# Loading the output weights of a decode kernel by transfers of 8 and 80 partitions instead of 128

## The chip, the cores and the metric

One Trainium2 chip, one of its cores. The metric is the device time of one execution in microseconds (us). The kernel before takes 1296.3 us (median; 1296.1 to 1296.4). The record sorts runs into a fast and a slow state.

## The reference, cut to what matters

One decode step of a transformer block: attention over a long cache, then a gated MLP. There are 4 sequences with one query each, 32 heads, 8192 cached positions, head size 128, model size 512, all bfloat16.

```
q = layernorm(x) @ wq                                 # 4 x 32 heads x 128
scores = q . k_cache / sqrt(128);  p = softmax(scores)
o = p . v_cache                                       # v_cache: 4 x 32 x 8192 x 128
h = x + o.reshape(4, 1, 4096) @ wo                    # wo: 4096 x 512, 4 MB
g, u = layernorm(h) @ w_gate, layernorm(h) @ w_up
h2 = h + (sigmoid(g) * u) @ w_down
```

The two caches are 512 MB together. The output weights `wo`, which the change is about, are 4 MB.

## The kernel before: the parts that matter

SyncE issues all large loads in one fixed order. K and V come in 4 MB loads into a ring of four slots, 128 partitions with 32 KB contiguous in each. `wo` reuses the buffer of the transposed keys, so it can only be loaded after the last score matmul, about 1220 us into the kernel, between the last V loads.

```
ring = SB("ring", [128, NS, TW], BF16)                 # NS = 4 slots of 32 KB per partition
kT = SB("kT", [128, 2, HT], BF16)
...
WD_PARTS = [(0, 5), (5, 10), (10, NFT)]
VL_PARTS = [(0, 64), (64, 96), (96, 128)]              # the last V load comes in three pieces
NWO = 8
HW = H // NWO                                          # 4 heads per transfer of wo
LAG2 = LAG // 2
items = [("wq", 0)]
for t in range(NT2 + LAG2):
    if t < NT2:
        items.append(("k", t))
    if t >= LAG2:
        items.append(("v", t - LAG2))
    for i in {LAG2 - 4: (0, 1), LAG2 - 3: (2, 3, 4), LAG2 - 2: (5, 6, 7)}.get(t - NT2, ()):
        items.append(("wo", i))
items += [("wg", 0), ("wu", 0), ("wd", 0)]
...
wo_v = kT[:, :, :].rearrange("p s f -> p (s f)").rearrange("p (h f) -> p h f", h=H)
...
    if kind == "wo":
        return [(lambda e: e.dma_start(
            wo_v[:, HW * t:HW * t + HW, :],
            A_wo.rearrange("(h p) f -> p h f", p=128)[:, HW * t:HW * t + HW, :]).then_inc(s_wo, 16),
            s_wo, 16 * NWO)]
...
for it in items:                                       # the order of issue on SyncE
    dma_of[it] = [P("sp", fn, (), sem, val) for fn, sem, val in load(it)]
...
# PE: all of wo but one sequence's last heads, then the last V load, then the rest
P("pe", lambda e: wo_mms(e, range(0, H - 8), 0, B, True), [otc_of[gl - 1], dma_of[("wo", NWO - 1)][0], d_xnT])
...
pe_pv(NST - 2, piece=0)
pe_pv(NST - 1, 0, 2, piece=1)
pe_pv(NST - 1, 2, 4, piece=2)
...
# wo waits for the last score matmul; the others for the last reader of their slot
op.deps = [sc_of[NST - 1]] if it[0] == "wo" else [consumed[p] for p in prev_of[it]]
```

A row of `wo` is 1 KB (512 numbers), so `wo` moves in 4096 packets of 1 KB; K and V move in packets of 32 KB.

## Time and profile before

| | |
|---|---|
| time, span of the profiled run | 1296.3 us, 1294.5 us |
| busy: DVE, PE | 48%, 39% |
| main DMA queue, share of 16 engines' span | 99.5% |
| `wo` issues | 8 of 512 KB, 32 packets on each engine |
| last V piece landed, last down-weight piece landed | 1277.4 us, 1291.1 us |

From the page of the kernel before: parts 3 (DMA queues) and 4 (the chain of waits).

```profile
q1 hardware_dynamic: 26016, 550.78, 99.5%
...
DMA 81%; PE 12%; SPq 4%; DVE 3%; issue 0%
DMA ring<-in_A_v_cache_dram 79%; PE PS L439 7%; PE PS L415 4%; SPq L220 2%; DVE kT L397 2%; SPq L236 1%; DMA ring<-in_A_wq_dram 1%; DMA ring<-in_B_w_down_dram 1%; SPq L228 1%; SPq L256 0%; PE PS L330 0%; DVE Lq L374 0%; DVE ring L347 0%; PE PS L357 0%; PE PS L637 0%
```

The kernel streams at what the DMA engines move, and 79% of its critical chain is V loads in flight. Everything that the change touches lies after 1220 us. The next view gives busy times in three stretches of that tail and one before it; the last two columns are the DMA engines' busy share and the GB/s moved.

```profile
core 0: us, PE busy (x) PEld busy (x) DVE busy (x) ACT busy (x) POOL busy (x), PEclk, DMA share, GB/s
1190.00:1220.00 30.00, 11.63 (x112) 3.73 (x116) 14.79 (x14) 0.00 (x0) 0.00 (x0) 0.56 1.01 432
1220.00:1245.00 25.00, 12.02 (x161) 5.96 (x153) 2.17 (x6) 3.62 (x7) 0.00 (x0) 0.64 0.96 390
1245.00:1270.00 25.00, 9.57 (x153) 4.59 (x154) 0.00 (x0) 0.00 (x0) 0.00 (x0) 0.50 1.01 391
1270.00:1295.00 25.00, 14.36 (x288) 9.99 (x285) 2.90 (x13) 1.91 (x4) 0.00 (x0) 0.50 0.75 286
```

The timeline of SyncE's queue before the change (start, duration of the issues, line, tiles, count). A long duration means that SyncE sat in the issue.

```profile
1220.42 0.94 SPq L220 DMA_DIRECT2D kT<-in_A_wo_dram  x2
1221.41 0.50 SPq L256 DMA_DIRECT2D ring<-in_A_v_cache_dram  x1
1221.95 22.66 SPq L220 DMA_DIRECT2D kT<-in_A_wo_dram  x3
1244.66 2.31 SPq L256 DMA_DIRECT2D ring<-in_A_v_cache_dram  x1
1247.01 6.84 SPq L220 DMA_DIRECT2D kT<-in_A_wo_dram  x3
1253.89 8.05 SPq L228 DMA_DIRECT2D ring<-in_A_v_cache_dram  x3
```

The single records of the trace add two readings. The semaphore of a 128-partition load receives 16 marks in the trace, read here as one from each engine that has finished its share: of the V load issued at 1200.9 us, seven land at 1226.6 to 1227.5, one at 1231.7 and eight at 1234.4 to 1236.4. So some engines run 8 us ahead of others. And packets have nearly fixed durations: 1.216 us for 32 KB, 46 ns for 1 KB (medians).

### The profile page before, as it was taken

The page shows a single profiled execution, that of the slowest core. Times are in us where ns is not written, and L with a number is a line of the kernel's source. Part 1 is how long each engine was busy: PE and PEld are TensorE (multiplying, and loading weights), DVE is VectorE, ACT ScalarE, POOL GpSimd, SP SyncE. Part 2 cuts the span into 40 slices and gives each one's busy share as a digit, 9 for nine tenths or more (in the row PEclk, how much of TensorE's full clock was granted, in tenths as well). Part 3 has the DMA queues.
Part 4 walks back from the last instruction along what each step waited for, and adds up shares of the span by engine and source line. Part 5 has one row for each costly group of instructions (what it writes and reads, how often), then busy time and mean ns, then how long its engine had stood idle before and what let it go on. Part 6 is the DMA issues. An engine that isn't in the chain of part 4 may idle for free.

```text
span 1294.5 us, 12693 instructions
## 1 busy us (share of the span) xinstructions
PE 499.5 (39%) x5827; PEld 193.4 (15%) x5827; DVE 625.4 (48%) x641; ACT 46.1 (4%) x102; POOL 10.6 (1%) x22
## 2 busy tenths in 40 slices
PE   3444334335244244334334334343343343343436
PEld 1011111112011021111111111011110111111114
DVE  5964644535544544535535435445535446445300
ACT  2000000000000000000000000000000000000000
POOL 3000000000000000000000000000000000000000
PEclk9996565665565565565666665665665665656655
DMA  9999999999999999999999999999999999999998
GB/s 405 434 428 432 432 428 433 431 430 430 433 431 430 433 429 431 433 427 433 434 426 434 431 427 435 429 431 435 425 434 432 426 435 428 431 434 429 429 376 322
DMA packets 26076, 551.58 MB, mean 426 GB/s; under 512 B 2340, under 2 KB 8232, under 8 KB 9256
## 3 DMA queue, kind: packets, MB, share of 16 engines
q1 hardware_dynamic: 26016, 550.78, 99.5%
q8 instruction: 45, 0.74, 0.2%
q14 instruction: 7, 0.06, 0.0%
q10 hardware_dynamic: 8, 0.00, 0.0%
HBM read 550.77 MB, written 0.00 MB: 425 GB/s over the span
## 4 chain that ended last, share of the span: by engine, by line
DMA 81%; PE 12%; SPq 4%; DVE 3%; issue 0%
DMA ring<-in_A_v_cache_dram 79%; PE PS L439 7%; PE PS L415 4%; SPq L220 2%; DVE kT L397 2%; SPq L236 1%; DMA ring<-in_A_wq_dram 1%; DMA ring<-in_B_w_down_dram 1%; SPq L228 1%; SPq L256 0%; PE PS L330 0%; DVE Lq L374 0%; DVE ring L347 0%; PE PS L357 0%; PE PS L637 0%
## 5 line engine op out<-in xcount | busy, mean ns | idle before, releaser
L397 DVE STREAM_TRANSPOSE kT<-ring 128x1024 uint32<-128x1024 uint32 x512 | 587.9, 1209 | 578.8 <-DMA ring<-in_A_k_cache_dram 578.6
L415 PE MATMUL PS<-kT,Lq 128*32 128x512 bf16 x2048 | 241.6, 619 | 563.3 <-DVE kT L397 443.8
L439 PE MATMUL PS<-ring,PTz 128*32 128x512 bf16 x2048 | 215.0, 564 | 208.7 <-DMA ring<-in_A_v_cache_dram 208.3
L415 PEld LDWEIGHTS PS<-kT,Lq 128*32 128x32 bf16 x2048 | 69.4, 135 | 692.4 <-DVE kT L397 471.9
L439 PEld LDWEIGHTS PS<-ring,PTz 128*32 128x32 bf16 x2048 | 64.5, 127 | 326.4 <-DMA ring<-in_A_v_cache_dram 197.1
L474 ACT ACTIVATE negm<-PS 128x1 f32<-128x1 f32 x16 | 2.7, 171 | 1156.3 <-PE PS L470 1156.3
L511 DVE TENSOR_SCALAR Zs<-PS,rinv 128x512 f32<-128x512 f32 x16 | 11.6, 723 | 36.4 <-PE PS L439 36.4
L506 ACT ACTIVATE PTz<-PS 64x512 bf16<-64x512 f32 x32 | 18.9, 592 | 16.5 <-PE PS L492 16.1
L518 PE MATMUL PS<-SelZ,Zs 128*128 128x8 f32 x128 | 19.1, 276 | 0.9 <-DVE Zs L511 0.9
L518 PEld LDWEIGHTS PS<-SelZ,Zs 128*128 128x128 f32 x128 | 17.6, 213 | 10.6 <-issue 8.9
L453 DVE TENSOR_REDUCE mx<-PS 128x1 f32<-128x512 f32 x16 | 10.5, 658 | 5.4 <-PE PS L415 5.4
L492 PEld LDWEIGHTS PS<-Sel,E_sb 128*32 128x32 bf16 x1024 | 10.4, 96 | 8.3 <-ACT E_sb L476 7.1
L492 PE MATMUL PS<-Sel,E_sb 128*32 128x32 bf16 x1024 | 11.0, 183 | 1.6 <-ACT E_sb L476 1.1
L476 ACT ACTIVATE E_sb<-PS,negm 128x512 bf16<-128x512 f32 x16 | 11.0, 688 | 0.5
L481 PEld LDWEIGHTS PS<-sig,Gsum 128*128 128x128 f32 x32 | 7.8, 305 | 12.6 <-issue 12.6
L481 PE MATMUL PS<-sig,Gsum 128*128 128x1 f32 x32 | 9.2, 356 | 0.0
L470 PEld LDWEIGHTS PS<-onesf,rowx 1*128 1x128 f32 x32 | 7.3, 281 | 13.0 <-issue 13.0
L470 PE MATMUL PS<-onesf,rowx 1*128 1x1 f32 x32 | 8.6, 336 | 0.0
L523 DVE CAST OT<-PS 128x8 bf16<-128x8 f32 x16 | 2.1, 132 | 11.6 <-PE PS L518 11.6
L347 DVE CAST ring<-PS 128x512 bf16<-128x512 f32 x4 | 2.5, 683 | 10.0 <-PE PS L330 10.0
L485 DVE RECIPROCAL rinv<-PS 128x1 f32<-128x1 f32 x16 | 2.1, 130 | 9.3 <-PE PS L481 9.3
L330 PE MATMUL PS<-ring,xnT 128*32 128x512 bf16 x32 | 3.6, 629 | 6.6 <-DMA ring<-in_A_wq_dram 6.6
(78 smaller groups left out, 81.3 us busy)
## 6 DMA issues: line engine op xcount, KB each, us to landing
ring<-in_A_k_cache_dram SPq DMA_DIRECT2D x64, 4096.0 KB, 29.7
ring<-in_A_v_cache_dram SPq DMA_DIRECT2D x63, 4096.0 KB, 34.0
ring<-in_A_wq_dram SPq DMA_DIRECT2D x1, 4096.0 KB, 12.3
kT<-in_A_wo_dram SPq DMA_DIRECT2D x8, 512.0 KB, 17.3
ring<-in_A_v_cache_dram SPq DMA_DIRECT2D x1, 2048.0 KB, 18.5
ring<-in_A_v_cache_dram SPq DMA_DIRECT2D x2, 1024.0 KB, 18.2
ring<-in_B_w_gate_dram SPq DMA_DIRECT2D x1, 1792.0 KB, 19.9
ring<-in_B_w_up_dram SPq DMA_DIRECT2D x1, 1792.0 KB, 23.5
```

What stands on the lines that cost most here:

```text
L220: return [(lambda e: e.dma_start(wo_v[:, HW * t:HW * t + HW, :], A_wo.rearrange("(h p) f -> p h f", p=128)[:, HW * t:HW * t + HW, :]).then ...
L228: return e.dma_start(ringv(slot)[:, c0:c1], kv_src(t, A_v_cache)[:, c0:c1]).then_inc(s_piece[i], 16)
L236: return e.dma_start(wd_v[:, t0:t1, :], B_w_down.rearrange("(t p) f -> p t f", p=128)[:, t0:t1, :]).then_inc(s_piece[3 + i], 16)
L397: return e.transpose(kT[:, buf, i * q:(i + 1) * q].bitcast(U32), ringv(src)[:, base + i * q:base + (i + 1) * q].bitcast(U32))
L415: mm = e.matmul(bS[g % 2][32 * j:32 * (j + 1), :], Lq[:, l0:l0 + 32], rhs, start=(s % GS == 0 and v == 0), stop=(s % GS == GS - 1 and v == 3),
L439: mm = e.matmul(bO[g % 2][32 * rq:32 * (rq + 1), :], PTz[:, g % 2, l0:l0 + 32], ringv(slot)[:, r0 * 128:(r0 + 4) * 128], start=(s % GS == ...
L470: p2_of[g] = P("pe", lambda e: e.matmul(bX[:, 0:1], rowx[0:1, :], onesf[0:1, 0:1], start=True, stop=True), [d2b_of[g], c_ones])
L481: L_of[g] = P("pe", lambda e: e.matmul(bX[:, 0:1], Gsum[:, :], sig[:, 0:1], start=True, stop=True), [exp_of[g], a1_of[g], d_g])
L492: mm = e.matmul(bP[g % 2][32 * a:32 * (a + 1), 32 * rr:32 * rr + 32], E_sb[:, 32 * rr:32 * rr + 32], Sel[:, a, :], start=True, stop=True, ...
L506: return e.activation(dst, src, ACT.Copy)
L511: z_of[g] = P("dve", lambda e: e.tensor_scalar(Zs[:, :], bO[g % 2][:, :], rinv[:, g % 2:g % 2 + 1], None, op0=ALU.mult), [pv_of[g * GS + G ...
L518: mm = e.matmul(bX[:, 256:264], Zs[:, 128 * r:128 * (r + 1)], SelZ[:, r, :], start=(r == 0), stop=(r == 3))
```

## The change

As its text and numbers suggest, the intent is to give one half of the engines more of `wo` than the other: 80 partitions are five shares of 16, while a transfer of 8 partitions can use 8 engines only.

```diff
-        NWO = 8
-        HW = H // NWO
+
+        WO_PARTS = [(0, 80, 8 * i, 8 * i + 8) for i in range(4)] + [(p, p + 8, 0, H) for p in range(80, 128, 8)]
+        NWO = len(WO_PARTS)
         LAG2 = LAG // 2
@@
-            for i in {LAG2 - 4: (0, 1), LAG2 - 3: (2, 3, 4), LAG2 - 2: (5, 6, 7)}.get(t - NT2, ()):
+            for i in {LAG2 - 4: (0, 1), LAG2 - 3: (2, 3, 4, 5, 6), LAG2 - 2: (7, 8, 9)}.get(t - NT2, ()):
@@
             if kind == "wo":
+                p0, p1, h0, h1 = WO_PARTS[t]
                 return [(lambda e: e.dma_start(
-                    wo_v[:, HW * t:HW * t + HW, :],
-                    A_wo.rearrange("(h p) f -> p h f", p=128)[:, HW * t:HW * t + HW, :]).then_inc(s_wo, 16),
+                    wo_v[p0:p1, h0:h1, :],
+                    A_wo.rearrange("(h p) f -> p h f", p=128)[p0:p1, h0:h1, :]).then_inc(s_wo, 16),
                     s_wo, 16 * NWO)]
```

Bytes, packets and everything on the other engines stay the same. Four transfers now move partitions 0 to 79 (8 heads each), six move 8 neighbouring partitions with all 32 heads.

## The prediction

> **What bounds it.** DMA throughput. Queue table: one queue takes 99.5% of 16 engines' span. Chain of waits: 81% DMA, 79% V loads. A 32 KB packet takes 1.213 to 1.22 us, so each DMA engine moves 27 GB/s, back to back. DVE (48%) and PE (39%) wait.
>
> Only the last 75 us can change. The 16 completion marks of each load, in the trace, show two groups of engines: of the V load issued at 1200.9 us, seven land at 1226.6-1227.5, one at 1231.7, eight at 1234.4-1236.4. In the tail the early group lacks work: busy engines drop from 16 to 9 at 1242-1245 (about 35 engine-us), because SyncE sits in the issue of output-weight transfers (11.3 us at 1221.95, 10.1 us at 1234.5 in the timeline). The last down-weight transfer ends at 1287 on the early eight, at 1289.4-1291.1 on the late eight; the kernel ends 3.3 us later.
>
> **What changes.** Same bytes; 8 issues become 10. Before, each engine moves 256 packets of 1 KB at 46 ns: 11.8 us. The Trainium skill, "DMA: Bandwidth & Descriptors", "Why a DMA increments its semaphore by 16 and not by 1", says the engine count is the largest one up to 16 that divides the outer dimension, the lowest-numbered. The 4-partition load of x fits in this trace: 4 data packets. So 80 partitions use 16 engines (160 packets each, 7.4 us), 8 partitions only engines 0-7 (192 more, 8.8 us). Engines 0-7: 16.2 us (+4.4). Engines 8-15: 7.4 us (-4.4). The intent must be that 0-7 are the early group, whose 8 us lead equals the difference (80% sure; no view numbers the engines). By engine time alone the idle gap fills, both groups end near 1287.5, and the gain is 3-4 us.
>
> **Against it.** The Trainium skill, "SBUF — State Buffer", "Door 1: The DMA port swizzle", says four adjacent partitions share one of 16 ports of 27.2 GB/s. No run here shows it yet. Each 8-partition transfer then puts four engines on each of two ports: 128 KB per port, 4.7 us instead of 1.47 us. Those ports (partitions 80-127) also take the late engines' V writes, and while engines 0-7 queue at two ports, their own stand idle. Six transfers: 17.6 us if the engines of a port stagger (two runs of three, six steps of 1.47 us each), 28 us in lockstep. With the 7.4 us that is 25 to 36 us for engines 0-7 instead of 11.8: +13 to +24. Less the idle gap (4.7 us), plus about 3 us for sharing with V: their end goes from 1287 to 1298-1309, past the old 1291.1. All of it is on the critical path: every later load on these engines (last V pieces, gate, up, down) queues behind it.
>
> **Prediction: 1304 us (+0.6%), 8 in 10 within 1293 to 1318. Faster by over 2%: 0.01; within 2%: 0.92; slower by over 2%: 0.07.**
>
> **What shows it.**
> - Unchanged until about 1220 us.
> - 8-partition transfers land 8 marks, not 16.
> - 1 KB packets take 100-190 ns while those transfers run; if 46 ns, the port argument is wrong and the time is near 1293.
> - The groups swap: engines with extra packets end last; GB/s in the last slices falls below 376 and 322.
> - The last V pieces land 5-15 us later than 1272-1277.
>
> **What would make it wrong.** No port limit, or buffering hides it: 1292-1294. Engines 0-7 are the late group: 1300 without port sharing, 1310-1320 with it. SyncE's blocked issues can move either way.

## The result

| | before | after |
|---|---|---|
| time, median | 1296.3 us | 1332.2 us (1329.2 to 1333.4, 4 runs) |
| ratio, 95% interval | | 1.0274 (1.0256 to 1.0291) |
| last mark of the last V piece | 1277.4 us | 1313.8 us |
| last mark of the down weights | 1291.1 us | 1327.4 us |
| median duration of a 32 KB packet, 1226 to 1263 us | 1.216 us | 1.938 us |
| median duration of a 1 KB packet, 1226 to 1300 us | 47 ns | 95 ns |

A ratio is the mean time of one kernel's fast runs over that of the other's of the same rounds, so it is not quite the ratio of the medians quoted.

The change made the kernel slower by 2.7%, outside the predicted range of 1293 to 1318 us. The 36 us are all there when the last V piece lands (1313.8 against 1277.4); what follows it is as long as before. The same stretches after the change, and one more:

```profile
1190.00:1220.00 30.00, 12.44 (x112) 3.89 (x116) 14.65 (x14) 0.00 (x0) 0.00 (x0) 0.56 1.00 431
1220.00:1245.00 25.00, 11.74 (x156) 5.18 (x149) 2.00 (x5) 3.62 (x7) 0.00 (x0) 0.57 1.06 298
1245.00:1270.00 25.00, 4.86 (x38) 2.24 (x38) 0.17 (x1) 0.00 (x0) 0.00 (x0) 0.56 0.92 189
1270.00:1295.00 25.00, 0.00 (x0) 0.00 (x0) 0.00 (x0) 0.00 (x0) 0.00 (x0) 0.50 0.80 198
1295.00:1331.00 36.00, 20.07 (x403) 13.54 (x403) 2.90 (x13) 1.91 (x4) 0.00 (x0) 0.50 0.75 265
```

The first line is as before. In the second the DMA engines are *more* busy than before (1.06 against 0.96) and move *less* (298 GB/s against 390). A busy DMA engine is one with a packet open; it says nothing of the rate. In the third the rate is half of before, and in the fourth PE has nothing to do for 25 us.

SyncE's queue after the change:

```profile
1220.31 0.89 SPq L222 DMA_DIRECT2D kT<-in_A_wo_dram  x2
1221.25 0.51 SPq L258 DMA_DIRECT2D ring<-in_A_v_cache_dram  x1
1221.81 41.74 SPq L222 DMA_DIRECT2D kT<-in_A_wo_dram  x5
1263.59 2.96 SPq L258 DMA_DIRECT2D ring<-in_A_v_cache_dram  x1
1266.59 23.33 SPq L222 DMA_DIRECT2D kT<-in_A_wo_dram  x3
1289.96 2.14 SPq L230 DMA_DIRECT2D ring<-in_A_v_cache_dram  x3
```

SyncE sits 41.7 us in five issues and 23.3 us in three, where before it had sat 22.7 us in three and 6.8 us in three. The last V load is issued at 1290.0 instead of 1253.9: 36 us later. From PE's timeline, two groups before the change, then the three with the longest waits after it (idle before, and what ended it, in brackets):

```profile
1263.07 3.60 PE L439 MATMUL PS<-ring,PTz 128*32 128x512 bf16 x32 [10.45 <-DMA ring<-in_A_v_cache_dram]
1267.64 3.55 PE L577 MATMUL PS<-OT,kT 128*128 128x4 bf16 x128 [0.97 <-DMA kT<-in_A_wo_dram]
```

```profile
1262.48 3.60 PE L441 MATMUL PS<-ring,PTz 128*32 128x512 bf16 x32 [16.23 <-DMA ring<-in_A_v_cache_dram]
1296.01 3.60 PE L441 MATMUL PS<-ring,PTz 128*32 128x512 bf16 x32 [29.93 <-DMA ring<-in_A_v_cache_dram]
1304.23 3.55 PE L579 MATMUL PS<-OT,kT 128*128 128x4 bf16 x128 [4.62 <-DMA kT<-in_A_wo_dram]
```

The longest waits of PE are for V (29.9 and 16.2 us), not for `wo` (4.6 us).

**A balance of the loss.** For each run I summed two things over the trace's DMA records after 1220 us, in engine-microseconds. *Excess* is the duration of all data packets above the usual one of their size (1216, 612, 309, 140 and 46 ns for 32, 16, 8, 3.5 and 1 KB). *Idle* is 16 engines' time without a packet (16 less the packets under way, wherever fewer than 16 are), up to the last weight packet.

```
               excess   idle    (sum - sum of before) / 16    end of the last weight packet
before           36.8   62.1                                   1290.7
after           491.4  195.9    36.8 us                        1326.9  (+36.3)
```

That the sum closes is bookkeeping (the bytes are the same); what it tells is the split. 455 of the 588 added engine-us, 28 us of time, are packets that take longer, and 134, 8 us, are engines without work. Of the excess over before, 185 lie on 32 KB packets and 57 on 16 KB packets, all of them V, which the change does not touch; 211 lie on the 1 KB packets.

### The profile page after: what moved, and what is told of

The parts are those of the page before. It is cut to its first block, busy times and chain, and to the rows that moved or that the text cites. A ratio compares the mean times of both kernels' runs of the same rounds, so it can differ in the third digit from the quotient of the medians.

```text
span 1330.8 us, 12695 instructions
## 1 busy us (share of the span) xinstructions
PE 502.1 (38%) x5827; PEld 193.5 (15%) x5827; DVE 625.4 (47%) x641; ACT 46.0 (3%) x102; POOL 10.6 (1%) x22
## 4 chain that ended last, share of the span: by engine, by line
DMA 82%; PE 12%; SPq 3%; DVE 3%; issue 0%
DMA ring<-in_A_v_cache_dram 80%; PE PS L441 7%; PE PS L417 4%; DVE kT L399 2%; SPq L222 2%; DMA ring<-in_B_w_down_dram 1%; SPq L238 1%; DMA ring<-in_A_wq_dram 1%; SPq L258 0%; PE PS L332 0%; DVE Lq L376 0%; SPq L230 0%; DVE ring L349 0%; PE PS L359 0%; PE PS L639 0%
## 5 line engine op out<-in xcount | busy, mean ns | idle before, releaser
L579 PE MATMUL PS<-OT,kT 128*128 128x4 bf16 (+2 forms) x160 | 4.6, 167 | 4.9 <-DMA kT<-in_A_wo_dram 4.6
## 6 DMA issues: line engine op xcount, KB each, us to landing
ring<-in_A_v_cache_dram SPq DMA_DIRECT2D x1, 2048.0 KB, 18.8
```

## The experiments

The theory at first is the one in the second half of the prediction, with the page that it names: four neighbouring partitions share a write port, and several engines at one port slow each other. The 4.7 us there is an estimate from that page's 27.2 GB/s. The rivals: (a) only the engine loads count, and the wrong half of the engines got more; (b) transfers on 8 engines are dear by themselves, because they fill those engines' queues and SyncE sits in their issue.

| run | edit, in words | us | ratio to before | excess | idle |
|---|---|---|---|---|---|
| e_spread | the six 8-partition transfers on partitions four or two apart | 1322.6 | 1.0202 | 387 | 172 |
| e_48 | 80 and 48 partitions, all on 16 engines | 1318.9 | 1.0171 | 396 | 94 |
| e_8only | 5/8 of the heads by 128 partitions, the rest by 8 neighbours | 1309.8 | 1.0102 | 151 | 165 |
| e_8spread | the same, 8 partitions four apart | 1303.1 | 1.0050 | 85 | 98 |
| e_act | the change, 8-partition transfers issued by ScalarE | 1327.2 | 1.0238 | 427 | 99 |
| e_before_act | before, `wo` issued by ScalarE | 1314.5 | 1.0140 | 30 | 68 |
| e_64 | 64 neighbouring partitions at a time | 1319.1 | 1.0174 | 398 | 70 |
| e_64s | 64 partitions, two apart, at a time | 1296.4 | 1.0000 | 37 | 65 |

The intervals of the ratios are within 0.0018 to either side. The argument rests on differences, all of which are well outside these intervals. All eight give correct results.

### e_probe: which engines does an 8-partition transfer use?

Before, plus four tiny loads behind a K load:

```diff
+            if t == NT2 - 2:
+                items += [("pr", i) for i in range(4)]
...
+            if kind == "pr":
+                return [(lambda e: e.dma_start(probe[0:1 << t, t, :], A_wo[0:1 << t, 0:64]
+                                               ).then_inc(s_probe[t], 16), s_probe[t], 16)]
```

> The kernel before with four tiny loads (1, 2, 4 and 8 partitions of 128 bytes) put behind K load 62, about 1181 us, to see which engines they ride on. Their marks come when each engine reaches them. If engines 0-7 are the early group, all of the 8-partition load's marks come within the early group's landings of the load ahead of it (7 early plus the one 4 us later); if they are the late group, all come some 8 us after. The 1-partition load tells which engine is number 0. Time 1296 to 1297 us.

Measured, from the marks in the trace (one run, 1296.3 us, unchanged; the loads were issued at 1162.5 to 1163.8 us, behind the load of 1162.2 us):

```
the load ahead of them   7 marks 1187.6-1188.7   1 at 1192.5   8 at 1195.6-1196.0
1 partition              1188.1
2 partitions             1188.3  1188.6
4 partitions             1187.8  1188.5  1188.8  1192.7
8 partitions             1188.0  1188.0  1188.7  1188.9  1189.0  1192.9  1195.8  1195.9
```

(Each load also has one mark at once, at 1163 to 1164 us, for the engines it does not use.) So the 8-partition load does use 8 engines, as the Trainium skill says ("DMA: Bandwidth & Descriptors", "Why a DMA increments its semaphore by 16 and not by 1"). But they are not one of the two groups: five are early, one is in between, two are late. Both alternatives of the prediction were wrong: moving work onto these 8 engines adds to two of the late ones.

### e_iso and e_iso2: single transfers by themselves

Two kernels of nothing but transfers, each waited for before the next (wrong results), each shape twice:

```diff
+                e.dma_start(W[80:88, 0:32, :], wo[80:88, 0:32, :]).then_inc(s[3], 16)
+                e.wait_ge(s[3], 16)
+                e.dma_start(W[96:128:4, 0:32, :], wo[96:128:4, 0:32, :]).then_inc(s[4], 16)
+                e.wait_ge(s[4], 16)
```

> Wrong result on purpose: only single transfers, each waited for before the next, each shape twice. Port theory: a 1 KB packet takes about 46 ns with 128 partitions and with 8 partitions four apart (one engine to a port), about 75 ns with 8 partitions two apart, about 150 ns with 8 neighbouring partitions (four engines to a port); the last needs near 5 us for 256 KB and the spread one near 1.5 us plus latency. The 80-partition and 48-partition transfers lie between (60 to 100 ns). 32 KB packets: 1.2 us spread, near 4.8 us for 8 neighbours. Rival (only the number of engines counts): 46 ns and 1.2 us everywhere.

> Wrong result on purpose: single transfers of 512 KB (one of 640 KB) of 1 KB packets, each waited for before the next, each shape twice, all on 16 engines. If a transfer's rows are dealt to the engines so that 64 partitions two apart put one engine on each port, these take as long as 128 partitions (about 2.3 us from first packet to last mark) with 46 ns packets, and the same for 32 partitions four apart; 64 neighbours and 32 neighbours (two engines to a port) take near 1.5 us more, with packets up to 90 ns. 16 partitions four apart or eight apart also reach only 8 ports and are as slow. If the number of partitions counts and not their ports: 32 and 16 partitions slow in every dealing.

Measured: time from the start of the first packet to the last mark, two repetitions, and the upper quartile of the 1 KB packets.

```
partitions                     KB    engines   us             75% of packets below
128                            512   16        2.30  2.36      46 ns
64, neighbours                 512   16        3.42  3.42      85 ns
64, two apart                  512   16        2.46  2.46      46 ns
32, neighbours                 512   16        3.39  3.63      82-87 ns
32, four apart                 512   16        2.36  2.40      46 ns
16, four apart                 512   16        3.74  3.64      96 ns
16, eight apart                512   16        3.60  3.60      91-93 ns
80, neighbours                 640   16        3.73  3.91      79 ns
48, neighbours                 384   16        3.43  3.33      94-114 ns
8, neighbours (80-87)          256    8        5.56  5.51      174-180 ns
8, two apart (80-94)           256    8        3.18  3.37      47-54 ns
8, four apart (96-124)         256    8        2.40  2.57      46 ns
8, neighbours (0-7)            256    8        6.12  5.53      175-193 ns
8, four apart (0-28)           256    8        2.45  2.54      46 ns
```

With 32 KB packets, 8 neighbours took 3.6 us per packet on average, 8 partitions four apart 1.6 to 1.7 us, and 128 partitions 1.29 to 1.32 us (1.213 us in the median). The order is the expected one, the sizes are not (4.8 and 1.2 us); why the packets of 8 partitions four apart took longer than 1.2 us is open.

The shapes come out as the port theory has them. The number of partitions does not count (32 four apart are as fast as 128); what does, by the port table, is how many engines meet at one port. No record names a port, and one rival was not tested apart: the rows picked in SBUF are the same rows in DRAM, so every dealing changes the source addresses too. Their spacing alone does not decide: 32 partitions four apart are fast and 16 four apart are slow, as the table has it (16 ports and 8). For 8 neighbours this is the 4.7 us per 256 KB that the prediction worked out from the Trainium skill ("SBUF — State Buffer", "Door 1: The DMA port swizzle"), instead of 1.47 us: 3.2 us more by the estimate, 2.9 to 3.2 us more measured for partitions 80 to 87 (5.5 against 2.4 to 2.6). The page's partition ranges (0 to 63 as slow as 0 to 31) agree too. Only the packets are less even than expected: not all at 150 ns, but a part at 46 and a part near 180.

### e_spread: same engines, same packets, other ports

```diff
+        WO_PARTS = [(0, 80, 1, 8 * i, 8 * i + 8) for i in range(4)] + [
+            (80, 96, 2, 0, H), (81, 96, 2, 0, H)] + [(p, 128, 4, 0, H) for p in range(96, 100)]
```

(with a third number, the step, in the slices of both sides)

> The changed kernel with the same six 8-partition transfers, same bytes, packets and engines, only the partitions dealt out differently: four transfers of 8 partitions four apart, two of 8 partitions two apart. Port theory: most of the loss of the 8-partition part goes, 1305 to 1318 us. Rival (transfers on 8 engines fill those engines' rings and SyncE sits in the issue, whatever the partitions): stays 1328 to 1334 us.

1322.6 us: 9.6 us of the 36 come back by nothing but dealing the partitions out differently. Rival (b) in its pure form falls. But the run lies above the expected range: most of the loss is not in the 8-partition transfers.

### e_48: all engines equal

```diff
+        WO_PARTS = [(0, 80, 1, 8 * i, 8 * i + 8) for i in range(4)] + [(80, 128, 1, 8 * i, 8 * i + 8) for i in range(4)]
```

(Behind the first two, the list of issues has `(2, 3, 4, 5)` and `(6, 7)` here, so as to fit the count of eight.)

> The changed kernel with the six 8-partition transfers replaced by four of 48 partitions (80 to 127, 8 heads each), so all 16 engines carry 256 packets each, as before the change. Port theory: the 80-partition half keeps its crowding and the 48-partition half has it too (8 partitions on each of four ports), 1300 to 1316 us. Rival (engine imbalance alone made the loss): 1296 to 1298 us.

1318.9 us, a little above the range. Every engine carries 256 packets of `wo` as before the change, and yet 22 us are lost: rival (a) falls as the sole cause. The prediction had costed the 80-partition part of this at nothing: it took these transfers at 46 ns per packet. How much of the 22 us is theirs and how much the 48-partition ones' was not run apart. In the trace of this run the 1 KB packets have a median of 88 ns, and 32 KB packets one of 1.899 us between 1226 and 1263 us. But the slowing is already there in the changed kernel before any 8-partition transfer is issued: its first one is issued at 1241.2 us, and from 1220 us until then 306 GB/s were moved instead of 411. At the 432 GB/s of the stretch before, that is some 5 us lost by then (my estimate). The V load issued at 1221 us lands at 1249.0 us before the change, at 1262.4 in the changed kernel and at 1263.8 in e_48.

### e_8spread and e_8only: the 8-partition transfers without the 80-partition ones

Heads 0 to 19 by five transfers of 128 partitions, heads 20 to 31 by 16 transfers of 8 partitions. The 8 engines carry the same 352 packets as in the changed kernel, the other 8 the same 160; the order of issue is fitted to the larger number of transfers (eight of the small ones ahead of V load 62, eight behind it).

```diff
 # e_8spread
+        WO_PARTS = [(0, 128, 1, 4 * i, 4 * i + 4) for i in range(5)] + [
+            (32 * b + a, 32 * b + 32, 4, 20, H) for b in range(4) for a in range(4)]
 # e_8only
+        WO_PARTS = [(0, 128, 1, 4 * i, 4 * i + 4) for i in range(5)] + [
+            (p, p + 8, 1, 20, H) for p in range(0, 128, 8)]
```

> Five eighths of the heads loaded as before by 128-partition transfers, three eighths by 16 transfers of 8 partitions four apart (12 heads each): the same 8 engines carry the same 352 packets as in the changed kernel, but no 80-partition transfer is left, and no two of a transfer's engines share a port. Sharing law from the 48-partition run (a packet written to a port that another engine is writing costs its 46 ns twice, once for each): only the 768 packets for partitions 64 to 127 share, 71 engine-us, 4.4 us, plus the 4.4 us of extra packets on 8 engines: 1299 to 1312 us. Rival (8-engine transfers are dear by themselves): 1315 us or more.

> The same as the run before it, with the 16 transfers on 8 neighbouring partitions each (four engines on each of two ports). Port theory: clearly dearer than the spread one, by 10 us or more, 1312 to 1335 us. Rival: equal to the spread one.

1303.1 us and 1309.8 us. So the 8-partition transfers cost 6.7 us even when each engine of a transfer has a port to itself (of which, by the balance, some 3 us are longer packets and some 2 us idle engines), and neighbours add 6.7 us to that; I had expected that addition to be 10 us or more and was wrong in size. The 13.4 us of e_8only are the same as the step from e_48 to the changed kernel (1332.2 - 1318.9 = 13.3). The two add up to the whole loss: 22.3 us for cutting `wo` at partition 80 (e_48 against the kernel before in its own rounds, 1296.6 us) and 13.4 us for the pieces of 8 neighbours. That they add up is a finding of size, not a proof that the two are independent, since e_8only cuts other heads and other partitions than the changed kernel.

e_8spread also shows who suffers. All its 8-partition transfers reach 8 ports, one engine to a port. The first eight move partitions 0 to 63, and the V packets beside them kept their time: the excess on 32 KB packets is 8.3 engine-us (before: 8.7), and all 18 V packets that start between 1244 and 1248.8 us, with these transfers under way, took 1.213 to 1.234 us. The last eight move partitions 64 to 127, into ports that, by the port table cited above, belong to other engines in a V load, and run while the 16 KB packets of the last V load do: these have an excess of 44.5 engine-us (before: 1.4), and the 52 that start between 1266 and 1270 us have a median of 1.146 us instead of 0.612. That the owner of the port is what makes the difference is an inference from the order of issue; no record names a port.

The trace also shows that this can't be the whole of it. From 1267 to 1271 us only 2.3 packets of 1 KB are under way on average, beside 14.1 V packets of 16 KB. If each V engine wrote only its own port, two or three of the 14 would suffer at most; but all 47 V packets that start there took 0.96 to 1.23 us. The changed kernel shows the same from 1273 to 1277 us: 2.3 packets of 1 KB under way, and all 29 V packets of 32 KB that start there took 1.57 to 2.69 us. Packets of 128-partition transfers do no such thing: in the kernel before, at 1266 to 1267 us, 1.8 of them are under way, and the 25 V packets that start there took 0.68 us at most. So a few engines with a narrow transfer slow nearly the whole stream. Through what, the runs do not show.

### e_64 and e_64s: halves, and every other partition

```diff
 # e_64
+        WO_PARTS = [(64 * (i % 2), 64 * (i % 2) + 64, 1, 8 * (i // 2), 8 * (i // 2) + 8) for i in range(8)]
 # e_64s
+        WO_PARTS = [(i % 2, 128, 2, 8 * (i // 2), 8 * (i // 2) + 8) for i in range(8)]
```

> The kernel before with its eight transfers cut by halves of the partitions (0 to 63, 64 to 127; 8 heads each) instead of by heads: all 16 engines, 256 packets each, as before. By the skill's port table and four neighbouring partitions per engine, half of the packets go to the engine's own port (the one it writes in a 128-partition transfer), half to another engine's. Sharing law (a packet on another engine's port costs 46 ns twice): 2048 packets, 188 engine-us, 12 us: 1305 to 1311 us. Rival (what counts is how many ports one transfer reaches, here only 8): as bad as the 80 and 48 split or worse, 1318 us or more.

> The same with even and odd partitions instead of halves: every transfer reaches all 16 ports, but seven eighths of the packets go to another engine's port. Sharing law: 3584 packets, 330 engine-us, 20.6 us: 1312 to 1321 us. Rival (number of ports reached): no loss, 1296 to 1299 us.

1319.1 us and 1296.4 us: both outside what I expected, and nearly exchanged. Both are what the rival says, that the number of ports that a transfer reaches is what counts. Both have 8 transfers of 64 partitions, 16 engines, 256 packets of 1 KB on each, the same order of issue. The halves cost 22.7 us; every other partition costs nothing (0.9984 to 1.0017). The part of my theory that fell is either how rows are dealt to engines (I took four neighbouring rows for each engine) or the law that a packet on another engine's port costs 46 ns twice; the two runs do not tell which. The stretches of e_64 and then of e_64s:

```profile
1220.00:1245.00 25.00, 12.22 (x162) 5.42 (x154) 2.00 (x5) 3.62 (x7) 0.00 (x0) 0.57 1.03 310
1245.00:1270.00 25.00, 4.59 (x37) 1.97 (x37) 0.17 (x1) 0.00 (x0) 0.00 (x0) 0.57 0.95 260
```

```profile
1220.00:1245.00 25.00, 12.98 (x165) 6.42 (x157) 2.17 (x6) 3.62 (x7) 0.00 (x0) 0.57 0.96 391
1245.00:1270.00 25.00, 8.84 (x145) 4.37 (x146) 0.00 (x0) 0.00 (x0) 0.00 (x0) 0.64 1.00 387
```

The DMA share is the same or higher, the rate is 310 and 260 GB/s against 391 and 387. In e_64s the packets keep their times (medians 1.216 us and 47 ns), in e_64 they nearly double (1.991 us and 88 ns). A simple sum fits e_64 and e_48 (and not e_64s): if each of the 4096 packets of `wo` takes 46 ns longer, and costs a V packet at the same port 46 ns too, that is 377 engine-us; both runs have 360 to 361 more excess than before. By themselves, such transfers cost only 1.0 us more each (3.4 against 2.4 us in e_iso2), by estimate 8 us for eight. The rest of the 22.7 us shows only in the company of V: V's own packets have 208 engine-us more excess than before, 13 us of time.

### e_act and e_before_act: the issue taken off SyncE

```diff
+        act_wo = []                            # SyncE's list loses these transfers
+        for i in range(first, NWO):            # first: 4 in e_act, 0 in e_before_act
+            (fn, sem, val), = load(("wo", i))
+            op = _Op("act", fn, ())
+            op.sem, op.val = sem, val
+            dma_of[("wo", i)] = [op]
+            act_wo.append((("wo", i), op))
...
         P("act", lambda e: e.activation(lnst[0:B, 9:10], lnst[0:B, 3:4], ACT.Sqrt), [exp_of[gl]])
+        for it, op in act_wo:
+            prog.ops["act"].append(op)
```

> The changed kernel with its six 8-partition transfers issued by ScalarE after its last exponential, so SyncE no longer waits in their issue and goes on with V. If the 134 engine-us of extra idle time come from SyncE's blocked issue, about 8 us go: 1320 to 1327 us, with the idle time near that of before. Rival (idle engines had nothing to do for want of bytes on them, whoever issues): 1329 us or more.

> The kernel before with its eight 128-partition transfers issued by ScalarE after its last exponential, SyncE free for V. The hole of about 35 engine-us at 1242 to 1247 us should close: 1293 to 1296 us. If it does not close, 1296 to 1298 us.

e_act: 1327.2 us, 0.2 us above the range. The idle time falls from 196 to 99 engine-us, so most of the added idle time goes when the 8-partition issues leave SyncE. The edit also puts these transfers on a queue of their own, from which an engine can take work while the other queue waits; the run does not tell the two apart, and SyncE still sat 24.6 us in one V issue. The last weight packet ends 10 us earlier (1316.7), but the kernel ends only 5 us earlier, since `wo` now lands later than needed: PE waits 6.9 us for it at the end.

e_before_act: 1314.5 us, a clear miss in time, though the hole did close: about 16 packets are under way from 1242 to 1246 us, where before there were 9 to 12. The loads end where they did before (last weight packet 1290.6 us), but `wo` itself lands at 1291.0 us instead of 1267.5, and PE's work on the last V load stands behind it:

```profile
1256.70 3.61 PE L446 MATMUL PS<-ring,PTz 128*32 128x512 bf16 x32 [6.58 <-DMA ring<-in_A_v_cache_dram]
1291.16 3.56 PE L584 MATMUL PS<-OT,kT 128*128 128x4 bf16 x128 [30.86 <-DMA kT<-in_A_wo_dram]
```

The Trainium skill ("DMA: Bandwidth & Descriptors", "Queues, rings and completion order") says that a DMA engine takes its queues in turn, packet by packet. This trace agrees: from 1236 to 1244 us, 105 packets of 1 KB start on ScalarE's queue and 99 of 32 KB on SyncE's, one for one, so the queue with the small packets gets little. Moving the issue to another queue is no free way to unblock SyncE.

No experiment beats the kernel before. e_before_act gives a hint: with the hole at 1242 us closed, its loads still ended at 1290.6 us, and its idle time is no smaller (68 against 62 engine-us); it has moved to the end, where from 1284 to 1289 us only 8 to 10 packets are under way.

## Why the prediction was wrong, point by point

- **What bounds the kernel; nothing changes before 1220 us.** Right: 432 and 431 GB/s in the stretch before.
- **80 partitions use 16 engines, 8 partitions use 8.** Right, by the marks.
- **"Engines 0-7 are the early group" (80%), else the late one.** Wrong in both branches. The 8 engines are five early, one between, two late (e_probe).
- **8 neighbouring partitions put four engines on each of two ports, 4.7 us instead of 1.47 us.** The size is right: 5.5 against 2.4 to 2.6 us, latency included, in e_iso (partitions 80 to 87). In a kernel such pieces cost 13.4 us (e_8only), at the lower end of the 13 to 24 us that the prediction allowed.
- **"With the 7.4 us": the 80-partition transfers at full rate.** This is the step that failed. They were taken at 46 ns per packet with no crowding, although the same page on ports applies to them. In the changed kernel, the 1 KB packets that start before any 8-partition transfer is issued have a median of 89 ns, and the 32 KB packets beside them (from 1225 us on) one of 1.69 us instead of 1.22. Cutting `wo` at partition 80, with all engines equal, costs 22.3 us (e_48, its 48-partition pieces included), more than the 8-partition transfers do (13.4 us).
- **"About 3 us for sharing with V".** Mis-sized. The excess on V's packets in the changed kernel is 242 engine-us above before, 15 us of time over 16 engines. What it left out is that V's own packets lengthen, and on nearly all engines at once (e_8spread).
- **"Less the idle gap (4.7 us)".** Wrong in sign. The hole at 1241 to 1248 us is 26 engine-us in the trace, not 35, and idle time grew by 134 engine-us (8 us) while SyncE sat longer in its issues; e_act removed 97 of them.
- **The signs.** 1 KB packets of 100 to 190 ns: half right (median 95, upper quartile 118 ns in the changed kernel). 8 marks: right. Last slices below 376 and 322 GB/s: right (192 and 272 in the last two). Groups that swap: wrong; 14 engines end the last transfer at 1323.0 to 1323.4 us, one at 1324.1, one at 1327.4. Last V pieces 5 to 15 us later: too small, 36 us.

What is shown: cutting a load by neighbouring partitions costs time where a cut with a step does not (e_64 against e_64s), it slows packets of `wo` and V alike, and 8-partition pieces add to it. What is argued: that the cause is the write ports; the table fits the shapes of e_iso and e_iso2, but source addresses changed with them, and what slows V packets on nearly all engines beside two narrow streams has no explanation here. What also stays open: which partitions each engine writes in an 80-partition transfer; and what exactly SyncE waits for while it sits in an issue.

## What to carry to other kernels

Before cutting a load by partitions, ask which partitions each piece reaches (by the port theory: which write ports), not only which engines carry it: pieces of 64 neighbouring partitions cost 22.7 us here, while pieces of 64 dealt out with a step of two cost nothing. Count the cost for the stream beside the transfer as well as for the transfer: here the stream's part was the larger one (208 of 361 engine-us in e_64). And do not take a busy DMA engine for a fast one: read GB/s and packet durations beside the busy share.

## What the Trainium skill lacked or had wrong

- "SBUF — State Buffer" (Door 1) tells of neighbouring ranges only and advises 32 over 64 partitions when 128 cannot be used. A step makes both as fast as 128: 64 two apart 2.46 us, 32 four apart 2.36 to 2.40 us, 128 partitions 2.30 to 2.36 us for 512 KB; neighbours 3.4 to 3.6 us.
- The same section, and the rules in "DMA: Bandwidth & Descriptors", tell what a narrow transfer loses itself, not what it costs the others (the second page's notes on back-pressure are about transfers between cores): beside transfers of 64 neighbouring partitions, the 32 KB packets of 128-partition loads went from 1.216 to 1.991 us, and two thirds of the loss of 22.7 us show only there (eight transfers alone lose 8 us, by estimate). Two engines with narrow transfers were enough to slow the packets of 14 others (e_8spread, 47 of 47 packets of 16 KB at 0.96 to 1.23 us, against 0.612 us).
- "DMA: Bandwidth & Descriptors" does not say how the rows of a SyncE-issued load are dealt to the engines for shapes other than 128 partitions. If it were four neighbouring rows for each engine with 64 partitions, e_64s should have lost 20.6 us by my sum; it lost none (ratio 1.0000), so that dealing or the sum is wrong.
- No page read for this has a duration for SyncE sitting in a single issue ("Perfetto Trace Analysis" says which steps the window of such an issue holds, not how long they can last): it was 16.3 us in one and 18.8 us in another in the changed kernel.
- "DMA: Bandwidth & Descriptors" names engines 7 and 15 as the usually slower ones, and ties its best guess at the cause to loads issued by GpSimd. It has nothing on what these SyncE-issued loads show: in e_probe, eight engines were 8 us behind seven others at 1188 us, and two of the eight that an 8-partition load uses were among them.
